# Delta-rule attention and a mixture of experts on one core: the expert stage in program order, with tokens fetched three tiles ahead and empty tiles behind branches

## The chip, the core and the metric

The kernel runs on one core of a Trainium2 chip. The core has five engines that run side by side: TensorE (PE, matrix products and transposes; its weight loads are shown apart as PEld), VectorE (DVE), ScalarE (ACT), GpSimd (POOL) and SyncE (SP), which here only issues transfers between the memory outside (DRAM) and the memory on the core. The metric is the device time of one execution in microseconds (us), as the median of several runs; lower is better.

## What is computed

There are two parts, one after the other. The first is attention by the delta rule, for 4 sequences of 768 tokens with 8 heads of width 48. The second sends each of the 4 x 768 = 3072 tokens (384 numbers each) to one of 8 experts and multiplies the result by a gate.

```python
# attention, for each sequence and head (state is 48 x 48)
k_n = k / (norm(k) + 1e-6)
for t in range(768):
    y[t] = q[t] @ state
    v_old = state.T @ k_n[t]
    state += beta[t] * outer(k_n[t], v[t] - v_old)
x = y with the heads side by side               # 3072 x 384

# experts: w1 is 8 x 384 x 1024, w2 is 8 x 1024 x 384, all float32
logits = (x / (norm(x) + 1e-6)) @ en.T / tau     # en: the expert vectors, normed
idx = argmax(logits);  gate = softmax(logits)[idx]
for e in range(8):
    m = idx == e
    out[m] = gate[m] * (maximum(x[m] @ w1[e], 0) @ w2[e])
```

With the reference's own inputs the experts get 385, 377, 351, 388, 365, 351, 421 and 434 tokens. In tiles of 128 tokens, each of one expert only, that makes 4 + 3 + 3 + 4 + 3 + 3 + 4 + 4 = 28 tiles.

## The kernel before

**Attention.** A sequence is cut into 12 chunks of 64 tokens; a unit is one chunk of two sequences (128 rows), so there are 24 units, number n = 2c + u. A unit's work is a list of steps, each with a place in a plan; a new unit starts every 20 places, so several are under way at once. PE, DVE, ACT and POOL run their instructions in the order of this plan.

**Routing.** The last steps of the plan find each token's expert, and write the token's number into that expert's list in DRAM (`idmap`). They are done for two chunks (G = 4 units, 512 tokens) at a time.

```python
    def route3(c, xc, ssx, lz):                     # place of each token in its expert's list
        oh = K["oh"]                                # oh: one-hot of the expert, 128 x G x E
        psR = K["psR"] = bank([128, G + 1, E])
        mm(psR, K["ones"][0:1, :], run.unsqueeze(1).broadcast_to([1, G + 1, E]))
        mm(psR[:, 0:G], K["mask_su"], oh, False)
        for g in range(G):
            mm(psR[:, g + 1:], K["ones"], oh[:, g:g + 1].broadcast_to([128, G - g, E]), False)
    # ... route4 makes slot_i and run (tokens so far of each expert) of psR;
    #     route5 and route6 make the gate and write x with it to x_dram

    def put_on_lists(g):                            # one such step for each of the G units
        def step(c, xc, ssx, lz):
            if g > 0:
                nc.gpsimd.memset(gap, 0.0)
            put = nc.gpsimd.indirect_dma_start(     # scatters 128 token numbers
                out=idmap[:, :], out_offset=bass.IndirectOffsetOnAxis(ap=K["slot_i"][:, g:g + 1], axis=0),
                in_=K["tokid"][:, c - 1 + g // NU, g % NU], in_offset=None)
            # ... the first of a group waits for those of the group before
```

**Experts.** The number of tiles of each expert is known only when the last tokens are routed, so `run` is turned into a table `info` of NT = 24 + 7 = 31 entries, the expert and the first list place of each tile, on one partition of DVE (some 20 small instructions). All 31 tiles are worked, those after the last used one with lists that hold only the number N, which names a row of zeros in x_dram and no row of the output.

```python
    def fetch(i):
        e = nc.values_load(info[0:1, 0, i:i + 1], engines=(SP,), min_val=0, max_val=E - 1)
        s = nc.values_load(info[0:1, 1, i:i + 1], engines=(SP,), min_val=0, max_val=NMAP - T)
        ids = mk.tile([128, ID], I32, name="ids", tag="ids", bufs=5)
        read = nc.sync.dma_start(ids, idmap[bass.ds(s, T), :])
        # ... after the last group's scatters into the lists
        w1 = wt.tile([128, KC, F], F32, name="w1", tag="w1")            # bufs=3
        nc.sync.dma_start(w1, moe_w1[bass.ds(e, 1)].rearrange("o (c p) f -> p (o c) f", p=128))
        w2 = wt.tile([128, NF, Dm], F32, name="w2", tag="w2")           # bufs=3
        nc.sync.dma_start(w2, moe_w2[bass.ds(e, 1)].rearrange("o (f p) m -> p (o f) m", p=128))
        x = mk.tile([128, ROW], F32, name="xg", tag="xg", bufs=5)
        nc.gpsimd.indirect_dma_start(out=x, ..., in_=x_dram[:, :], ...) # gathers 128 rows by ids
        return ids, w1, w2, x

    def transposed(x):                              # 3 transposes on PE, a copy on DVE
        ...
    def experts(xT, ids, w1, w2, x):
        hT = mk.tile([128, NF, T], F32, name="hT", tag="hT")
        for f in range(0, NF, 4):                   # NF = 8, KC = 3
            psH = acc([128, 4, T])
            for i in range(4):
                for j in range(KC):
                    nc.tensor.matmul(psH[:, i, :], lhsT=w1[...], rhs=xT[:, j, :], ...)
            nc.scalar.activation(hT[:, f:f + 4, :], psH, ACT.Relu)
        psO = acc([128, Dm])
        for f in range(NF):
            nc.tensor.matmul(psO, lhsT=hT[:, f, :], rhs=w2[:, f, :], ...)
        y = mk.tile([128, Dm], F32, name="y", tag="y", bufs=4)
        nc.vector.tensor_scalar_mul(y, psO, x[:, Dm:Dm + 1])
        nc.gpsimd.indirect_dma_start(out=out[:, :], ..., in_=y, ...)    # scatters 128 rows by ids

    ahead = [fetch(0), fetch(1)]
    xT = transposed(ahead[0][-1])
    for i in range(NT):
        now = ahead.pop(0)
        if i + 2 < NT:
            ahead.append(fetch(i + 2))
        nxT = transposed(ahead[0][-1]) if ahead else None
        experts(xT, *now)
        xT = nxT
```

In this text hidden(i) is the first product of tile i with its Relu, result(i) the second with its scaling and scatter, and w1(i), w2(i), ids(i), x(i) are what the tile reads.

Of the kernel before, what the change touches and what calls it, by code (L numbers as in the profile page):

```python
# [16 lines left out]
C = 64  # L17
# [5 lines left out]
def kernel(  # L23
# [53 lines left out]
    base_e = cpool.tile([1, E], F32, name="base_e")  # L77
    K = {}
# [181 lines left out]
    def late_constants3():  # L260
# [17 lines left out]
                          none.broadcast_to([128, NMAP * ID // 128 // NONE, NONE]))  # L278
        zrow = ac.tile([1, ROW], F32, name="zrow")
        nc.vector.memset(zrow, 0.0)  # L280
        nc.sync.dma_start(x_dram[N:N + 1, :], zrow)

# [22 lines left out]
    outs = {}  # L305
# [157 lines left out]
    def outputs(U):  # L463
        c, u = U["c"], U["u"]
        if u == 0 and c % 2 == 0:
            outs[c // 2] = (XC[c // 2 % 2],
                            wk.tile([128, 2, NU], F32, name="ssx", tag="ssx"),
                            wk.tile([128, 2, NU, E], F32, name="lz", tag="lz"))
        xc, ssx, _ = outs[c // 2]
        p = apply(U["M"], U["Z"])  # L470
        U["x"] = xc[:, c % 2, u, 0:Dm]
        xh = U["x"].rearrange("p (h d) -> p h d", h=H)
        if c > 0:
            nc.vector.tensor_tensor(xh, p, U["Yq"], op=ALU.add)
        else:
            nc.vector.tensor_copy(xh, p)
        ysq = wk.tile([128, Dm], F32, name="ysq", tag="ysq", bufs=1)
        nc.scalar.activation(ysq, U["x"], ACT.Square, accum_out=ssx[:, c % 2, u:u + 1])
# [8 lines left out]
    def logits(U):  # L487
        p = bank([128, E])
        for j in range(KC):
            for i in range(2):  # L490
                mm(p[HALF[i]], U["xT"][:, j, HALF[i]], enT[:, j, :], j == 0)
        nc.vector.tensor_copy(outs[U["c"] // 2][2][:, U["c"] % 2, U["u"]], p)

    G = 2 * NU
    ge = [128, G, E]

    def small(name, shape):
        return wk.tile(shape, F32, name=name, tag=name)

    def last_of_two_chunks(f):  # L500
        return lambda U: f(U["c"], *outs[U["c"] // 2]) if U["n"] % G == G - 1 else None

    def route1(c, xc, ssx, lz):

        ssx = ssx.rearrange("p o u -> p (o u)")
        nc.gpsimd.tensor_tensor(out=ssx, in0=ssx, in1=half.rearrange("p u h -> p (u h)")[:, 0:G], op=ALU.pow)
        lz = lz.rearrange("p o u e -> p (o u) e")
        m = small("m", [128, G])
        nc.vector.tensor_reduce(m, lz, axis=AX.X, op=ALU.max)
        K["el"] = small("el", ge)  # L510
        nc.vector.tensor_tensor(K["el"], lz, m.unsqueeze(2).broadcast_to(ge), op=ALU.subtract)

    def route2(c, xc, ssx, lz):

        pref = K["pref_e"].broadcast_to(ge)
        oh = K["oh"] = small("oh", ge)
        nc.vector.scalar_tensor_tensor(out=oh, in0=K["el"], scalar=0.0, in1=pref, op0=ALU.is_equal, op1=ALU.mult)
        best = small("best", [128, G])
# [3 lines left out]
    def route3(c, xc, ssx, lz):  # L522


        oh = K["oh"]
        psR = K["psR"] = bank([128, G + 1, E])
        mm(psR, K["ones"][0:1, :], run.unsqueeze(1).broadcast_to([1, G + 1, E]))
        mm(psR[:, 0:G], K["mask_su"], oh, False)
        for g in range(G):
            mm(psR[:, g + 1:], K["ones"], oh[:, g:g + 1].broadcast_to([128, G - g, E]), False)  # L530

    def route4(c, xc, ssx, lz):

        psR = K["psR"]
        rk = small("rk", ge)
        nc.vector.tensor_tensor(rk, psR[:, 0:G], K["oh"], op=ALU.mult)
        nc.vector.tensor_copy(run, psR[0:1, G])
        K["slot_i"] = wk.tile([128, G], I32, name="slot_i", tag="slot_i")
        slot = small("slot", [128, G])
        nc.vector.tensor_reduce(slot, rk, axis=AX.X, op=ALU.add)  # L540
        nc.vector.tensor_copy(K["slot_i"], slot)

    def route5(c, xc, ssx, lz):
        ssx = ssx.rearrange("p o u -> p (o u)")
        nc.vector.tensor_scalar_add(ssx, ssx, 1e-6)
        nc.vector.reciprocal(ssx, ssx)
        nc.vector.tensor_tensor(K["el"], K["el"], ssx.unsqueeze(2).broadcast_to(ge), op=ALU.mult)
        nc.scalar.activation(K["el"], K["el"], ACT.Exp)

    def route6(c, xc, ssx, lz):  # L550

        gate = xc.rearrange("p o u d -> p (o u) d")[:, :, Dm:Dm + 1]
        den = small("den", [128, G])
        nc.vector.tensor_reduce(den, K["el"], axis=AX.X, op=ALU.add)
# [3 lines left out]
        for o in range(2):  # L558
            t0 = (c - 1 + o) * C
            for i in range(2):  # L560
                nc.sync.dma_start(xd[i, t0:t0 + C], xc[HALF[i], o])
# [4 lines left out]
    def put_on_lists(g):  # L566
# [3 lines left out]
        def step(c, xc, ssx, lz):  # L570
            if g > 0:
                nc.gpsimd.memset(gap, 0.0)
            put = nc.gpsimd.indirect_dma_start(
                out=idmap[:, :], out_offset=bass.IndirectOffsetOnAxis(ap=K["slot_i"][:, g:g + 1], axis=0),
                in_=K["tokid"][:, c - 1 + g // NU, g % NU], in_offset=None)
            if g == 0:
                for other in lists[-G:]:
                    tc.add_manual_dep(put.ins, other.name, AFTER, reason="tokens' lists: two chunks after two others")
            else:
                tc.declare_no_dep(put.ins, group=f"lists{c}", reason="tokens' lists: distinct places")  # L580
            tc.add_to_no_dep_group(f"lists{c}", put.ins)
            lists.append(put.ins)
        return last_of_two_chunks(step)
# [14 lines left out]
        (79, x_transposes), (82, logits), (84, last_of_two_chunks(route1)), (87, last_of_two_chunks(route2)),  # L598
        (91, last_of_two_chunks(route3)), (94, last_of_two_chunks(route4)), (98, last_of_two_chunks(route5)),
        (103, last_of_two_chunks(route6)),  # L600
# [8 lines left out]
    ]  # L609
    steps = [(U["n"] * PERIOD + at, i, U["n"]) for U in UNITS for i, (at, _) in enumerate(PLAN) if i or U["n"]]  # L610
# [9 lines left out]
    wt = ctx.enter_context(tc.tile_pool(name="wt", bufs=3))  # L620
    mk = ctx.enter_context(tc.tile_pool(name="mk", bufs=2))
    pe = ctx.enter_context(tc.tile_pool(name="pe", bufs=1, space=bass.MemoryType.PSUM))

    def acc(shape):
        return pe.tile(shape, F32, name="acc", tag="acc", bufs=8)


    thr_i = cpool.tile([1, E, N // T], I32, name="thr_i")
    nc.gpsimd.iota(thr_i, pattern=[[0, E], [T, N // T]], base=0, channel_multiplier=0)
    thr = cpool.tile([1, E, N // T], F32, name="thr")  # L630
    nc.vector.tensor_copy(thr, thr_i)
    nth_i = cpool.tile([1, NT, 1], I32, name="nth_i")
    nc.gpsimd.iota(nth_i, pattern=[[1, NT], [0, 1]], base=0, channel_multiplier=0)
    nth = cpool.tile([1, NT, 1], F32, name="nth")
    nc.vector.tensor_copy(nth, nth_i)
# [4 lines left out]
    nc.vector.tensor_reduce(tiles[:, 0, :], thr, axis=AX.X, op=ALU.add)  # L640
    ends = cpool.tile([1, 1, E], F32, name="ends")
# [17 lines left out]
    nc.vector.tensor_copy(info[:, 1, :], begin)  # L659


    def fetch(i):
        e = nc.values_load(info[0:1, 0, i:i + 1], engines=(SP,), min_val=0, max_val=E - 1)
        s = nc.values_load(info[0:1, 1, i:i + 1], engines=(SP,), min_val=0, max_val=NMAP - T)
        ids = mk.tile([128, ID], I32, name="ids", tag="ids", bufs=5)
        read = nc.sync.dma_start(ids, idmap[bass.ds(s, T), :])
        for put in lists[-G:]:
            tc.add_manual_dep(read.ins, put.name, AFTER, reason="tokens' lists are complete")
        w1 = wt.tile([128, KC, F], F32, name="w1", tag="w1")
        nc.sync.dma_start(w1, moe_w1[bass.ds(e, 1)].rearrange("o (c p) f -> p (o c) f", p=128))  # L670
        w2 = wt.tile([128, NF, Dm], F32, name="w2", tag="w2")
        nc.sync.dma_start(w2, moe_w2[bass.ds(e, 1)].rearrange("o (f p) m -> p (o f) m", p=128))
        x = mk.tile([128, ROW], F32, name="xg", tag="xg", bufs=5)
        nc.gpsimd.indirect_dma_start(
            out=x, out_offset=None, in_=x_dram[:, :],
            in_offset=bass.IndirectOffsetOnAxis(ap=ids[:, 0:1], axis=0))
        return ids, w1, w2, x

    def transposed(x):
        xT = mk.tile([128, KC, T], F32, name="xTm", tag="xTm", bufs=3)  # L680
        psX = acc([128, KC, 128])
        for j in range(KC):
            nc.tensor.transpose(psX[:, j, :], x[:, j * 128:(j + 1) * 128], ident)  # L683
        nc.vector.tensor_copy(xT, psX)
        return xT

    def experts(xT, ids, w1, w2, x):
        hT = mk.tile([128, NF, T], F32, name="hT", tag="hT")
        for f in range(0, NF, 4):
            psH = acc([128, 4, T])  # L690
            for i in range(4):
                for j in range(KC):
                    nc.tensor.matmul(psH[:, i, :], lhsT=w1[:, j, (f + i) * 128:(f + i + 1) * 128], rhs=xT[:, j, :],  # L693
# [50 lines left out]
```

## Time and profile before

The time before is 832.64 us (median of 3 runs, 830.83 to 836.68). The profiled execution spans 831.9 us from the first to the last instruction, with a mean granted TensorE clock of 0.970 of full speed.

| engine | busy us | share of the span | instructions |
|---|---|---|---|
| PE | 731.6 | 88% | 15196 |
| PEld | 622.3 | 75% | 15196 |
| DVE | 280.3 | 34% | 632 |
| ACT | 243.8 | 29% | 468 |
| POOL | 226.7 | 27% | 260 |

A row of a group in the profile reads: line, engine, operation, what it writes <- what it reads, size, count; then busy time in all, mean ns of one, idle time of the engine just before these instructions and what ended it. The rows of 40 digits cut the span into 40 slices of 20.8 us; a digit is the busy share in tenths. In the timeline a row is: start in us, duration in us, engine, line, operation, what it writes <- what it reads, count, and in brackets the idle time before and what ended it. "DMA" rows count the 16 transfer engines of the core; "landing" is when a transfer is complete. A float32 matrix product shows as two records in PE's rows.

### The profile page before, as it was taken

The numbers are of one execution on the slowest core, as the hardware profiler recorded it, in microseconds if no ns is written. First come the engines' busy times: TensorE is split into PE (matmuls) and PEld (weight loads), VectorE is DVE, ScalarE is ACT, GpSimd is POOL, SyncE is SP. The second block draws the span as 40 slices with busy tenths as digits, with TensorE's granted clock in tenths as the row PEclk, the third lists the DMA queues.
The fourth block names the chain that finished last, engine by engine and source line by source line (L and its number), as shares of the span: only waits on it lengthen the run. The fifth ranks groups of instructions, "written<-read, shape, count | busy, mean of one in ns | idle before, by whom it ended". The sixth has DMA issues, their size and how long they took to land. (4 is left out here: it accounts for less than half of the span.)

```text
span 831.9 us, 33270 instructions
## 1 busy us (share of the span) xinstructions
PE 731.6 (88%) x15196; PEld 622.3 (75%) x15196; DVE 280.3 (34%) x632; ACT 243.8 (29%) x468; POOL 226.7 (27%) x260
## 2 busy tenths in 40 slices
PE   3589989999999989999886079999999999999995
PEld 2478878888888888888775067778888887777784
DVE  5565555555555655555432201100111111111000
ACT  3445444454445444454332001111111101101110
POOL 5543224433433433441200211111111111111110
PEclk9999999999999999999988579999999999999998
DMA  6344211321312321110010799999999999999920
GB/s 114 58 120 76 42 32 33 84 51 33 74 34 45 70 52 24 22 46 5 5 44 2 258 360 329 330 329 321 329 329 324 322 312 337 330 316 331 336 98 0
DMA packets 134957, 132.19 MB, mean 159 GB/s; under 512 B 84154, under 2 KB 119393, under 8 KB 134818
## 3 DMA queue, kind: packets, MB, share of 16 engines
q1 hardware_dynamic: 129874, 118.76, 46.9%
q0 software_dynamic: 4736, 11.27, 3.6%
q8 instruction: 119, 1.95, 1.0%
q14 instruction: 20, 0.16, 0.1%
q10 hardware_dynamic: 208, 0.05, 0.0%
HBM read 118.39 MB, written 13.04 MB: 158 GB/s over the span
## 5 line engine op out<-in xcount | busy, mean ns | idle before, releaser
L693 PE MATMUL acc<-xTm,w 128*128 128x128 f32 x1488 | 173.5, 277 | 0.0
L693 PEld LDWEIGHTS acc<-xTm,w 128*128 128x128 f32 x1488 | 171.0, 194 | 0.3
L698 PE MATMUL acc<-w,hT 128*128 128x384 f32 x496 | 165.1, 486 | 0.0
L698 PEld LDWEIGHTS acc<-w,hT 128*128 128x128 f32 x496 | 91.9, 190 | 57.5
L695 ACT ACTIVATE hT<-acc 128x512 f32<-128x512 f32 x62 | 37.0, 597 | 323.1 <-PE acc L693 291.9
L700 DVE TENSOR_SCALAR y<-acc,xg 128x384 f32<-128x384 f32 x31 | 19.1, 618 | 305.6 <-PE acc L698 305.6
L701 POOL DMA_INDIRECT out_dram<-y,ids x31 | 31.6, 1018 | 270.4 <-DVE y L700 270.4
L398 DVE COPY_PREDICATED P<-below,pair 128x512 f32<-128x512 int32 x96 | 70.0, 731 | 49.4 <-PE pair L308 42.2
L308 PE MATMUL pair<-W,P 64*64 64x64 f32 x3072 | 75.5, 224 | 12.5 <-issue 8.0
L384 ACT ACTIVATE W<-pair 128x512 f32<-128x512 f32 x96 | 57.5, 599 | 91.9 <-PE pair L308 86.5
L308 PEld LDWEIGHTS pair<-W,P 64*64 64x64 f32 x3072 | 64.3, 136 | 17.5 <-issue 11.4
L323 POOL TENSOR_TENSOR rn<-rn,half 128x8 f32<-128x8 f32 x24 | 39.5, 1644 | 137.1 <-DVE rn L322 103.9
L308 PE MATMUL bank<-Z,G 64*64 64x48 f32 x1536 | 57.9, 220 | 7.3 <-issue 5.9
L308 PE MATMUL bank<-R,W 64*64 64x48 f32 x1536 | 56.2, 218 | 6.6 <-issue 4.5
L308 PEld LDWEIGHTS bank<-Z,G 64*64 64x64 f32 x1536 | 51.8, 136 | 8.3 <-issue 5.9
L308 PEld LDWEIGHTS bank<-R,W 64*64 64x64 f32 x1536 | 51.2, 135 | 8.8 <-issue 8.2
L368 PE MATMUL bank<-ident,W 128*128 128x128 f32 x288 | 47.9, 289 | 1.3 <-ACT W L384 1.2
L308 PE MATMUL pair<-T,AJ 64*64 64x64 f32 x1536 | 39.0, 226 | 9.9 <-DVE T L376 7.0
L362 POOL TENSOR_TENSOR G<-G,upper 128x512 f32<-128x512 f32 x24 | 30.9, 1287 | 37.2 <-ACT G L356 36.2
L308 PEld LDWEIGHTS pair<-T,AJ 64*64 64x64 f32 x1536 | 31.7, 135 | 12.2 <-DVE T L376 7.8
L683 PEld LDWEIGHTS acc<-ident,xg 128*128 128x128 f32 x93 | 12.3, 145 | 36.4 <-issue 23.5
L683 PE MATMUL acc<-ident,xg 128*128 128x128 f32 x93 | 16.0, 283 | 26.5 <-DMA xg<-x_dram,ids 26.5
(161 smaller groups left out, 879.4 us busy)
## 6 DMA issues: line engine op xcount, KB each, us to landing
w<-in_moe_w_dram SPq DMA_DIRECT2D x62, 1536.0 KB
x_dram<-XC SPq DMA_DIRECT2D x24, 200.0 KB
k_in<-in_k_dram SPq DMA_DIRECT2D x48, 96.0 KB
QQ<-in_q_dram SPq DMA_DIRECT2D x48, 96.0 KB
v_in<-in_v_dram SPq DMA_DIRECT2D x48, 96.0 KB
idmap<-none SPq DMA_DIRECT2D x1, 1792.0 KB
ids<-idmap SPq DMA_DIRECT2D x31, 8.0 KB
xg<-x_dram,ids POOLq DMA_INDIRECT x31
```

What stands on the lines that cost most here:

```text
L308: nc.tensor.matmul(out_, lhsT=lhsT, rhs=rhs, start=start, stop=True, skip_group_check=True)
L323: nc.gpsimd.tensor_tensor(out=U["rn"], in0=U["rn"], in1=half[:, 0], op=ALU.pow)
L362: nc.gpsimd.tensor_tensor(M, M, upper.broadcast_to(hc), op=ALU.mult)
L368: nc.tensor.transpose(p[:, j].rearrange("p r c -> p (r c)"), src[:, j].rearrange("p r c -> p (r c)"), ident)
L384: nc.scalar.activation(out_, in_, ACT.Copy)
L398: nc.vector.copy_predicated(U["P"], below[s].broadcast_to(jc), p)
L683: nc.tensor.transpose(psX[:, j, :], x[:, j * 128:(j + 1) * 128], ident)
L693: nc.tensor.matmul(psH[:, i, :], lhsT=w1[:, j, (f + i) * 128:(f + i + 1) * 128], rhs=xT[:, j, :], start=(j == 0), stop=(j == KC - 1))
L695: nc.scalar.activation(hT[:, f:f + 4, :], psH, ACT.Relu)
L698: nc.tensor.matmul(psO, lhsT=hT[:, f, :], rhs=w2[:, f, :], start=(f == 0), stop=(f == NF - 1))
L700: nc.vector.tensor_scalar_mul(y, psO, x[:, Dm:Dm + 1])
L701: nc.gpsimd.indirect_dma_start(out=out[:, :], out_offset=bass.IndirectOffsetOnAxis(ap=ids[:, 0:1], axis=0), in_=y, in_offset=None, bounds_ ...
```

## The change

The change is in the order and the timing of the work between the last routing steps and the end. Each expert tile that is worked does the same arithmetic as before.

1. **The last two chunks are routed one by one** (groups of 2, 2, 2, 2, 2, 1, 1 chunks). The last group has then two units, and two scatters into the lists, where it had four.
2. **Weights of expert 0 are loaded during attention**, into buffers that are never shared with attention's, by 14 transfers of 192 or 256 KB, one for each unit's 20 places of the plan from place 100 on. Tile 0 is taken to be expert 0's first tile (the number of tiles of expert 0 is at least 1 now), so its list place needs no table.
3. **Two constant tables** of the count (`thr`, `nth`) are made during attention.
4. **The whole expert stage is in program order** on every engine, SP's transfers too, with buffers taken in turn from rings. ids are read five tiles ahead, x three tiles ahead, w1(i + 3) is asked for after hidden(i) and w2(i + 3) after result(i). PE's order is hidden(i), transposes of tile i + 1, result(i).
5. **The first weights from DRAM**, w1(1), are asked for only once x(0) has landed.
6. **Empty tiles behind branches**: tiles 0 to 23 are always worked, 24 to 27 only if more than 24 tiles are used, 28 to 30 only if more than 28 are. Every engine loads the number of used tiles into a register.

```diff
+    w1_first = cpool.tile([128, KC, F], F32, name="w1_first")
+    w2_first = cpool.tile([128, NF, Dm], F32, name="w2_first")
...
+    def first_weights(i):
+        if i < NF:
+            nc.sync.dma_start(w2_first[:, i], moe_w2[0, i * 128:(i + 1) * 128])
+        else:
+            c, f = (i - NF) // 2, (i - NF) % 2 * (F // 2)
+            nc.sync.dma_start(w1_first[:, c, f:f + F // 2], moe_w1[0, c * 128:(c + 1) * 128, f:f + F // 2])
...
+    groups, group_of = [], []
+    while len(group_of) < NC:
+        chunks = 1 if len(group_of) >= NC - 2 else 2
+        groups.append(dict(n=len(groups), first=len(group_of), chunks=chunks))
+        group_of += chunks * groups[-1:]
...      (route1 to route6 and put_on_lists work on a group g of G = 2 * chunks units)
+    events += [(PERIOD * (5 + i), lambda i=i: first_weights(i)) for i in range(NF + 2 * KC)]
...
+    ctx.enter_context(tc.manual_schedule())
...
+    w1_ring = ring("w1_", 3, [128, KC, F], first=[w1_first])
+    w2_ring = ring("w2_", 3, [128, NF, Dm], first=[w2_first])
+    ids_ring, x_ring = ring("ids", 7, [128, ID], I32), ring("xg", 6, [128, ROW])
...      (where, read_ids, read_x, read_w1, read_w2, transposed, hidden, result: fetch and experts in pieces)
+    where(work[0], 0)                    # no table: e = 0, s = 0
+    work[0].w1, work[0].w2 = w1_ring(), w2_ring()
+    read_ids(work[0])
+    read_x(work[0])
...      (the table info is made of run, as before)
+    nc.vector.tensor_scalar_max(tiles[:, :, 0], tiles[:, :, 0], 1.0)
...
+    for i in range(1, 5):
+        where(work[i], i)
+        read_ids(work[i])
+        if i == 1:
+            tc.add_manual_dep(read_w1(work[i]).ins, work[0].read.ins.name, AFTER, reason="first tokens, then weights")
+            read_w2(work[i])
+        if i < 3:
+            read_x(work[i])
+    read_w1(work[2])
+    read_w2(work[2])
+    transposed(work[0])
+    count = nc.values_load(used[0:1, 0:1], min_val=0, max_val=NT)
+
+    def work_through(first, last):
+        for i in range(first, last):
+            if i + 3 < NT:
+                read_x(work[i + 3])
+            hidden(work[i])
+            if i + 3 < NT:
+                read_w1(work[i + 3])
+            if i + 1 < NT:
+                transposed(work[i + 1])
+            result(work[i])
+            if i + 3 < NT:
+                read_w2(work[i + 3])
+            if i + 5 < NT:
+                where(work[i + 5], i + 5)
+                read_ids(work[i + 5])
+
+    parts = [N // T, N // T + E // 2, NT]
+    work_through(0, parts[0])
+    with tc.If(count > parts[0]):
+        work_through(parts[0], parts[1])
+        with tc.If(count > parts[1]):
+            work_through(parts[1], parts[2])
...
-    ahead = [fetch(0), fetch(1)]
-    xT = transposed(ahead[0][-1])
-    for i in range(NT):
-        ...
```

## Prediction

> **What bounds the kernel now.** I read the page's rows of 40 slices first, for the stages:
>
> ```profile
> PE   3589989999999989999886079999999999999995
> PEclk9999999999999999999988579999999999999998
> DMA  6344211321312321110010799999999999999920
> ```
>
> There are two stages with a hole between them. In slices 0 to 21 (attention, to about 455 us) PE is busy and the transfer engines have much room; slice 22 (458 to 478 us) has no matrix product at all; from there to the end PE is at 9 and the transfers are at 9 too. The change touches the hole and the second stage, so I cut these into windows (window in us, its length, then busy us and count for each engine, PE clock, DMA share, GB/s):
>
> ```profile
> 464.00:468.00 4.00, 0.00 (x0) 0.00 (x0) 0.00 (x0) 0.00 (x0) 0.36 (x1) 0.50 0.41 99
> 468.00:474.00 6.00, 0.00 (x0) 0.00 (x0) 0.00 (x0) 0.00 (x0) 0.63 (x1) 0.50 1.04 401
> 483.00:496.35 13.35, 13.35 (x70) 11.18 (x69) 0.58 (x2) 1.19 (x2) 0.94 (x1) 0.81 1.05 387
> 496.35:821.90 325.55, 325.12 (x2007) 259.72 (x2005) 32.05 (x59) 35.83 (x60) 1.00 0.89 300
> ```
>
> From 496.35 us on PE has 325.12 us of work in 325.55: it is the bound there, with 30 tiles, 10.85 us each. The transfers run at 300 GB/s against 387 to 401 when they are behind, so they are near the bound but not on it. The timeline gives the hole's steps and one steady tile:
>
> ```profile
> 456.68 1.04 POOL L573 DMA_INDIRECT idmap<-tokid,slot_i  x1 [4.84 <-DVE ssx L545]
> 458.02 0.95 POOL L573 DMA_INDIRECT idmap<-tokid,slot_i  x1 [0.21 <-issue]
> 459.28 0.96 POOL L573 DMA_INDIRECT idmap<-tokid,slot_i  x1 [0.22 <-issue]
> 460.55 0.96 POOL L573 DMA_INDIRECT idmap<-tokid,slot_i  x1 [0.22 <-issue]
> 464.55 0.38 SPq L666 DMA_DIRECT2D ids<-idmap  x1
> 467.64 0.98 POOL L674 DMA_INDIRECT xg<-x_dram,ids  x1 [6.14 <-issue]
> 474.04 0.88 PE L683 MATMUL acc<-ident,xg 128*128 128x128 f32 x3 [18.35 <-DMA xg<-x_dram,ids]
> 482.64 0.90 PE L683 MATMUL acc<-ident,xg 128*128 128x128 f32 x3 [7.72 <-DMA xg<-x_dram,ids]
> 483.33 7.80 PE L693 MATMUL acc<-xTm,w 128*128 128x128 f32 x48
> ...
> 507.31 5.52 PE L693 MATMUL acc<-xTm,w 128*128 128x128 f32 x48
> 512.66 5.33 PE L698 MATMUL acc<-w,hT 128*128 128x384 f32 x16
> ...
> 816.76 5.33 PE L698 MATMUL acc<-w,hT 128*128 128x384 f32 x16
> ...
> 823.02 0.98 POOL L701 DMA_INDIRECT out_dram<-y,ids  x1 [9.51 <-DVE y L700]
> ```
>
> The hole is a chain: four scatters into the lists, 1.27 us apart; the last ends at 461.5 and lands about 3 us later, which releases ids(0) at 464.55; x(0) is gathered from 467.64 and reaches PE at 474.04, 6.4 us, while four weight transfers fill the DMA (share 1.04). Then PE has x(0) but stands in program order before the transposes of x(1), which come at 482.64. So hidden(0) begins at 483.33, 31.3 us after the last logits are copied (452.05). At the other end the last product is done at 822.1, and SP's waits show what follows (engine, line, what it waited for: us in total, times, longest):
>
> ```profile
> SPq L739 <- DMA out_dram<-y,ids: 34.7, 1, 34.7
> SPq L739 <- PEq L739: 6.1, 2, 5.6
> ```
>
> SP issued its last transfer at about 790.3, so the last scatter lands near 825.0, 3 us after PE; the remaining 6.9 us to 831.9 are the common end.
>
> [...] clock 0.50 in the hole, hidden(0) takes 7.80 us where a steady one takes 5.52. The new kernel will pay this once too. [...] Here the list scatters land in 3.1 us (median); the shorter last group thus saves the issue of two scatters and no landing. [...]
>
> **The change part by part.**
>
> *Empty tiles.* 28 tiles are used. No expert's count lies just under a multiple of 128 (377 is nearest to 384 from below), so rounding cannot make a 29th; 385 and 388 could at most drop one. "More than 24" is true, "more than 28" is false: tiles 28 to 30 fall away, 3 x 10.85 = **-32.6 us** of PE time in the stage where PE is the bound.
>
> *Routing.* Two scatters fewer: -2 x 1.27 = -2.5. Of route3's twelve records for four units (0.65 + 0.64 + 1.85 us) half of the eight of 1.85 go: -0.9. Against it, chunk 10's own routing falls into the draining attention: some 14 DVE instructions of about 0.2 us and 8 PE records. DVE is a fifth busy there (2.13 of the 10 us from 440), so I charge 1 us, not their sum of 3. Net -2.4: ids(0) at about 462.1.
>
> *ids(0) needs no table.* The table was ready at about 461.7, before the scatters had landed, so this alone is worth nothing; in program order the table's instructions now come after the gate's, end near 463, and delay only ids(1), which is not urgent.
>
> *x(0) alone on the DMA.* ids(0) to gather 3.1 as before: 465.2. The gather without weights beside it: 205 KB, a link like the scatters, so I estimate 3.5 instead of 6.4: x(0) at 468.7. Transposes 0.9 and copy 0.6 as at 474.04 to 475.56: hidden(0) can begin at **470.2**, since its weights are there and no x(1) stands before it: 13.1 earlier than 483.33. The register load of the count lies in PE's order between the transposes and hidden(0), beside the copy.
>
> *Tile 0* takes 13.1 us as before (483.33 to 496.45), as the clock is low again: hidden(1) at 483.3. w1(1) and w2(1), 3.1 MB from 468.7 at 387 GB/s, take 8.1 us: there at 477 to 478, in time. w1(2) and w2(2) follow by 487, needed from 494. In the steady state a weight buffer is asked for again at the same point as before (w1 after hidden of the tile that used it) and needed 27 us later, as before. So no gain and no loss from the ring; x is one tile earlier.
>
> *Steady tiles.* Same products, another order; PE was never waiting, so 10.85 stays. Tiles 1 to 27 end at 483.3 + 325.6 - 32.6 = 776.3.
>
> *Branches.* Two compares, the second behind PE's last work: +1.
>
> *End.* w1(30) and w2(30) are asked for although tile 30 is not worked; w2(30) only after result(27), just when y goes out. 1.5 MB at 387 GB/s are 4.1 us beside the last scatter. Contended scatters land in 7.2 us (median of all 31; lowest 3.0): **+4.2**.
>
> *Loads during attention.* 3.1 MB more, over some 250 us in which the DMA is about 20% busy: 0.
>
> Sum: 831.9 - 13.1 - 32.6 + 1 + 4.2 = 791.4 for the profiled span. The timed runs lie 0.7 above it (832.64 against 831.9): **792**.
>
> **Rivals.**
> 1. *The branches hold all engines together.* If each block begins only when earlier work is done, PE would lose its lead at tile 24[...]. For it: nothing inside a branch can be moved ahead of it[...]. Against: each engine has the number in its own register, and needs no other engine to decide.
> 2. *The transfers become the bound.* With PE 13 us earlier and the first weights asked for later (468.7 instead of 465.2), tiles 1 to 3 could wait. For it: the DMA share is 0.89 even in the steady part, and small gathers then land late. Against: 3.1 MB per 10.85 us is 290 GB/s, and 387 was reached. Two or three waits of 2 us: 796 to 798.
> 3. *The chain is longer than I think at its start.* If chunk 10's routing holds up unit 23 by its full 3 us, or its scatters hold the first of the last group: 794 to 796.
> 4. *The end is free.* If the unused weights don't slow the scatter, and x(0) lands in 2.5 us: 787.
>
> **Range and chances.** The sure part is the skipped tiles; the start has four estimates of 1 to 2 us each, the end one of 4, the branches one of 0 to 10. That is why the range reaches farther up: 784 to 803. The -32.6 alone is 3.9%; to lose the 2%, stalls of 29 us would be needed, which only a slower steady tile (+1 us each) could make. Faster 0.95, same 0.03, slower 0.02.
>
> **What would show it.** Right: L573's last scatter near 458; x(0) at PE near 469; the first product of the experts near 470 with the clock at 0.5; 28 pairs of products, 10.85 us apart, without idle PE at tile 24; the last near 776; the last scatter landing some 7 us after it. Wrong: an idle PE ahead of the first product of tile 24 (rival 1); PE waiting for w in tiles 1 to 3 (rival 2); the last logits later than 453 (rival 3); 31 tiles worked.

## The result, and the profile after

| | before | after |
|---|---|---|
| device time, median of 4 runs each, us | 832.43 | 799.98 |
| ratio, with its 95% interval | 1 | 0.9606 (0.9555 to 0.9657) |
| span of the profiled run, us | 831.9 | 798.6 |

The change makes the kernel 3.9% faster: 32.5 us, where 40 were predicted. The rows of 40 slices of the changed kernel (20 us each):

```profile
PE   2578899998999998999988729999999999999993
PEclk9699999999999999999999658999999999999997
DMA  6336422321142131111001029999999999999996
```

The hole has not gone. It is at slice 23 and ends at 480 us, only 3.6 us earlier than before, and PE's clock is already down in slice 22, while attention still works. The copy of the last logits, before and after:

```profile
452.05 0.17 DVE L492 COPY lz<-bank 128x8 f32<-128x8 f32 x1 [2.04 <-PE bank L308]
```

```profile
463.25 0.17 DVE L511 COPY lz<-bank 128x8 f32<-128x8 f32 x1 [2.40 <-PE bank L325]
```

From there on the timeline of the changed kernel has the same steps as the one shown of before:

```profile
468.26 0.96 POOL L605 DMA_INDIRECT idmap<-tokid,slot_i  x1 [0.21 <-issue]
...
472.21 2.41 SPq L692 DMA_DIRECT2D ids<-idmap  x2
474.72 0.99 POOL L698 DMA_INDIRECT xg<-x_dram,ids  x1 [5.49 <-DMA ids<-idmap]
...
478.12 0.87 PE L714 MATMUL acc<-ident,xg 128*128 128x128 f32 x3 [12.16 <-DMA xg<-x_dram,ids]
...
479.70 7.71 PE L723 MATMUL acc<-xTm,w_first 128*128 128x128 f32 x48 [0.70 <-DVE xTm L715]
...
492.73 5.52 PE L723 MATMUL acc<-xTm,w 128*128 128x128 f32 x48
...
780.45 5.33 PE L730 MATMUL acc<-w_first,hT 128*128 128x384 f32 x16
...
786.71 1.02 POOL L733 DMA_INDIRECT out_dram<-y,ids  x1 [8.56 <-DVEq L806]
```

From these rows and the same ones of before, each link, in us:

| link | before | after | difference | predicted |
|---|---|---|---|---|
| start to last logits copied | 452.05 | 463.25 | **+11.2** | +1.0 |
| last logits to ids(0) asked for | 12.5 | 9.0 | -3.5 | -3.4 |
| ids(0) to the gather of x(0) | 3.1 | 2.5 | -0.6 | 0 |
| gather to the transposes of tile 0 | 6.4 | 3.4 | -3.0 | -2.9 |
| transposes to hidden(0) | 9.3 | 1.6 | -7.7 | -7.8 |
| hidden(0) to hidden(1) | 13.1 | 13.0 | -0.1 | 0 |
| hidden(1) to the last product | 325.6 | 293.05 | -32.6 | -32.6, and +1 for branches |
| last product to the end | 9.8 | 12.8 | +3.0 | +4.2 |
| sum | 831.9 | 798.6 | -33.3 | -40.5 |

All links of the hole and of the expert stage came out within 0.6 us of what was worked out (the one us for branches aside, which is not there), the end at 3.0 us instead of 4.2. One link did not: attention's last logits are 11.2 us late, ten more than was charged. The experiments are about that, and about the 3 us of the end.

### The profile page after: what moved, and what is told of

The parts are those of the page before. It is cut to its first block, busy times and chain, and to the rows that moved or that the text cites. A ratio compares the mean times of both kernels' runs of the same rounds, so it can differ in the third digit from the quotient of the medians.

```text
span 798.6 us, 32885 instructions
## 1 busy us (share of the span) xinstructions
PE 705.7 (88%) x15002; PEld 603.9 (76%) x15002; DVE 281.7 (35%) x644; ACT 240.6 (30%) x463; POOL 223.9 (28%) x257
## 3 DMA queue, kind: packets, MB, share of 16 engines
q8 instruction: 119, 1.95, 1.0%
## 4 chain that ended last, share of the span: by engine, by line
PE 58%; DMA 17%; issue 12%; DVE 6%; ACT 5%; SPq 0%; POOL 0%; POOLq 0%; ACTq 0%; DVEq 0%
PE pair L325 19%; DMA out_dram<-y,ids 16%; PE bank L325 15%; PE acc L723 8%; PE acc L730 7%; PE bank L385 6%; ACT G L373 2%; PE bank L360 1%; PE bank L501 1%; ACT W L401 1%; DVE P L415 1%; DVE W L376 1%; ACT KT L401 1%; DVE XC L492 1%; PE acc L714 1%
## 5 line engine op out<-in xcount | busy, mean ns | idle before, releaser
L725 ACT ACTIVATE hT<-acc 128x512 f32<-128x512 f32 x56 | 33.5, 598 | 279.9 <-PE acc L723 264.7
L723 PEld LDWEIGHTS acc<-xTm,w 128*128 128x128 f32 x864 | 99.3, 192 | 4.8
L723 PE MATMUL acc<-xTm,w 128*128 128x128 f32 x864 | 99.4, 275 | 0.0
L730 PE MATMUL acc<-w,hT 128*128 128x384 f32 x288 | 95.9, 486 | 0.0
L733 POOL DMA_INDIRECT out_dram<-y,ids x28 | 28.5, 1017 | 228.6 <-DVE y L732 211.5
L325 PE MATMUL pair<-W,P 64*64 64x64 f32 x3072 | 75.6, 224 | 13.3 <-issue 8.3
L730 PEld LDWEIGHTS acc<-w,hT 128*128 128x128 f32 x288 | 53.3, 190 | 33.4
L715 DVE COPY xTm<-acc 128x384 f32<-128x384 f32 x29 | 16.2, 558 | 151.9 <-PE acc L714 151.9
L723 PEld LDWEIGHTS acc<-xTm,w_first 128*128 128x128 f32 x480 | 57.2, 198 | 3.5 <-DVE xTm L715 1.1
L723 PE MATMUL acc<-xTm,w_first 128*128 128x128 f32 x480 | 57.4, 281 | 0.7 <-DVE xTm L715 0.7
L730 PE MATMUL acc<-w_first,hT 128*128 128x384 f32 x160 | 53.3, 486 | 0.0
L325 PE MATMUL pair<-T,AJ 64*64 64x64 f32 x1536 | 40.5, 228 | 11.1 <-DVE T L393 7.0
```

Of the source, the lines that this page charges most:

```text
L325: nc.tensor.matmul(out_, lhsT=lhsT, rhs=rhs, start=start, stop=True, skip_group_check=True)
L715: nc.vector.tensor_copy(t.xT, psX)
L723: nc.tensor.matmul(psH[:, i, :], lhsT=t.w1[:, j, (f + i) * 128:(f + i + 1) * 128], rhs=t.xT[:, j, :], start=(j == 0), stop=(j == KC - 1))
L725: nc.scalar.activation(t.hT[:, f:f + 4, :], psH, ACT.Relu)
L730: nc.tensor.matmul(psO, lhsT=t.hT[:, f, :], rhs=t.w2[:, f, :], start=(f == 0), stop=(f == NF - 1))
L733: nc.gpsimd.indirect_dma_start(out=out[:, :], out_offset=bass.IndirectOffsetOnAxis(ap=t.ids[:, 0:1], axis=0), in_=y, in_offset=None, bound ...
```

## Experiments

All runs of one group were on one chip; the groups are e1 to e4, the changed kernel again to e7, and e8 to e11. The kernel before took 821.0, 818.9 and 835.2 us on their chips, so ratios to it are compared, not times. Attention also differs from trace to trace of one program: the logits of unit 19 came at 405.2 us in one trace of the changed kernel and at 388.6 in another, on another chip. Therefore the traces are compared over short stretches. The stretches of all traces, in us ("clock falls": how long before the last logits the last halving of PE's clock ahead of them begins). In the traces of the kernel before and of the changed one every stretch at one clock, apart from the last, is a whole multiple of 3.41 us long (before: 6.83 us from 416.41 at 0.50, then 27.31 at 1.00, then 37.55 at 0.50, so 2, 8 and 11 of them); two traces whose clock falls 3 us apart can differ by one such step.

| kernel | logits of unit 1 | unit 21 to 23 | clock falls | last logits to ids(0) | hidden(0) to (1) | end | ratio |
|---|---|---|---|---|---|---|---|
| before | 93.6 | 14.4 | 1.5 | 12.5 | 13.1 | 9.8 | 1 |
| after | 96.4 | 21.9 | 16.7 | 9.0 | 13.0 | 12.8 | 0.9606 |
| e1 pairs | 99.3 | 15.1 | 3.9 | 12.0 | 12.8 | 11.8 | 0.9544 |
| e2 weights in the hole | 93.4 | 21.0 | 15.4 | 8.9 | 13.6 | 12.3 | 0.9563 |
| e3 no unused weights | 98.9 | 21.6 | 16.8 | 9.0 | 12.9 | 11.0 | 0.9569 |
| e4 all tiles | 99.0 | 21.0 | 15.4 | 9.0 | 13.7 | 9.8 | 0.9900 |
| after again | 96.1 | 21.3 | 16.3 | 9.0 | 13.2 | 12.9 | 0.9603 |
| e5 pairs, spread | 92.7 | 15.6 | 5.0 | 12.0 | 13.9 | 11.9 | 0.9506 |
| e6 filled drain | 96.1 | 19.5 | 13.1 | 8.4 | 13.3 | 12.5 | 0.9548 |
| e7 all of it | 94.1 | 17.9 | 9.7 | 12.7 | 11.0 | 11.0 | 0.9481 |
| e8 moved routing | 99.0 | 18.1 | 8.5 | 9.0 | 13.7 | 12.2 | 0.9550 |
| e9 pairs, best | 92.9 | 16.7 | 8.5 | 12.0 | 12.5 | 11.0 | 0.9497 |
| e10 moved, best | 93.5 | 18.1 | 8.3 | 9.0 | 11.0 | 11.0 | **0.9447** |
| e11 no branch | 97.6 | 21.7 | 16.4 | 9.0 | 13.2 | 9.6 | (one run) |

### e1: the last two chunks routed together again

```diff
-        chunks = 1 if len(group_of) >= NC - 2 else 2
+        chunks = 2
```

> The changed kernel with its last two chunks routed together again (last group 4 units, 4 scatters). Theory R (chunk 10's own routing, put into PE's and DVE's order of the draining attention, costs more than the two scatters save): the last logits are copied near 456 to 458 instead of 463.25, because the 8 route records and the PSUM bank they hold no longer stand ahead of units 22 and 23; from there to ids(0) 12.5 us as in the kernel before instead of 9.0; sum about 796 to 798. Theory C (the clock fell by chance of its window, routing or not): last logits near 463 still, and 3.5 us later ids(0): 803 to 804. Either way the halving of the clock relative to the last logits shows in the trace: C says some 16 us before them again, R says at most 5 us before.

Measured: ratio 0.9544 (0.9504 to 0.9584). Units 21 to 23 take 15.1 us instead of 21.9, and the clock falls 3.9 us before the last logits instead of 16.7. The way from there to ids(0) is 3.0 us longer. So routing the last chunks one by one costs 6.8 us and brings 3.0: this part of the change loses some 4 us by the traces. (Against e2 to e4, on e1's own chip, it costs 5.9 to 6.5 us.) The ratio points the same way, by 5 us, but its interval and the changed kernel's overlap. The two traces show how. First the timeline of the kernel before, PE alone:

```profile
440.81 1.10 PE L308 MATMUL bank<-Z,G 64*64 64x48 f32 x32
441.77 1.14 PE L308 MATMUL bank<-R,W 64*64 64x48 f32 x32
```

and the same two groups (the output of unit 22, the first solve of unit 23) in the changed kernel, with the route products of chunk 10 ahead of them:

```profile
444.67 0.40 PE L325 MATMUL bank<-run,ones 1*128 1x24 f32 x2
...
445.76 1.32 PE L325 MATMUL bank<-Z,G 64*64 64x48 f32 x32
...
447.74 0.14 DVE L567 COPY run<-bank 1x8 f32<-1x8 f32 x1
...
447.88 1.95 PE L325 MATMUL bank<-R,W 64*64 64x48 f32 x32 [0.80 <-DVE run L567]
```

The first group waits for the route products in PE's order. The second needs a PSUM bank; there are two, and the route's result holds one until DVE has read it, which in DVE's order comes after unit 22's output. The solve starts 2.1 us after the output's products instead of 1.0. From the logits of unit 21 to this solve it is 6.5 us instead of 4.2: +2.3. Then the same 32 records take 1.95 us instead of 1.14: at 446.55 the clock was halved, and the remaining 15.4 us to the last logits had taken 10.3 before: +5.1. Sum 7.4, the whole difference between 14.4 and 21.9. Of the 5.1 us, 4.3 are PE's own records, busy for 11.12 us instead of 6.87; the other 0.8 are longer waits.

### e2: tile 0's weights loaded in the hole

```diff
-    events += [(PERIOD * (5 + i), lambda i=i: first_weights(i)) for i in range(NF + 2 * KC)]
...
-    work[0].w1, work[0].w2 = w1_ring(), w2_ring()
     read_ids(work[0])
+    read_w1(work[0])
+    read_w2(work[0])
```

> The changed kernel with tile 0's weights not loaded during attention, but asked for right after ids(0), as in the kernel before. Theory D (those 14 transfers, which all ran between 63 and 89 us, are what makes attention 3.8 us later at unit 20): logits of unit 20 near 401.5 instead of 405.2, and the lost head start costs 3 to 6 us in the hole: 799 to 802. Rival (attention is late by its clock and by chance, the transfers are free): unit 20 near 404 to 406 still, hidden(0) begins 3 to 6 us later than in the changed kernel: 803 to 806.

(The figures 401.5 and 405.2 of this text belong to unit 19.) Measured: ratio 0.9563 (0.9529 to 0.9597), not told apart from the changed kernel's; it makes 796 of 832.4 us, below both forecasts. Unit 1's logits come at 93.4 us instead of 99, unit 19's at 390.5, against 396.4 to 402.6 in e1, e3 and e4 on the same chip. From ids(0) to hidden(0) it is 11.0 us instead of 7.5: the gather of x(0), which now has weights beside it, takes 6.7 us of it instead of 3.4. So the early weights bring 3.5 us in the hole, and unit 1 is 5.5 us later with them (3.0 in the changed kernel's own trace): as done here, that part of the change shows no gain. Theory D holds at unit 1. That its delay lasts to the end of attention is not shown, as the second group has unit 19 both early and late with the same loads (see e5).

### e3, e4, e11: the end and the branches

e3 asks for the weights of tiles 28 to 30 only inside the last branch; e4 works all 31 tiles without branches; e11 is e3 with 28 tiles in line, and leaves tiles 28 to 30 out altogether.

```diff
     # e3
-            if i + 3 < NT:
+            if i + 3 < last or last < parts[1]:
                 read_w1(work[i + 3])       # and read_w2 in the same way
...
         with tc.If(count > parts[1]):
+            for t in work[parts[1]:]:
+                read_w1(t)
+                read_w2(t)
     # e4
-    work_through(0, parts[0])
-    with tc.If(count > parts[0]):
-    ...
+    work_through(0, NT)
```

> The changed kernel, but the weights of tiles 28 to 30 are asked for inside the last branch, so that no unused ones are read. Theory (w2(30) beside the last scatter makes the end 12.8 us instead of 9.8): the end from the last product to the last instruction falls to about 10, total 797 to 798. Rival (the end is longer for the branch or because this scatter really writes 50 rows): the end stays at 12 to 13 us, 800.

> The changed kernel without branches: all 31 tiles are worked, in line. Theory (the skipped tiles give their full 3 x 10.85 us and the branches cost nothing): 800 + 32.6 - about 2 to 3 (no unused weights at the end) = 829 to 831. If the branches cost something, the difference to the changed kernel is smaller by it: each us of branch cost lowers this figure by one. It is also a second sample of the same attention: last logits near 463 if the routing does it, 455 to 460 if the clock fell by chance.

> e3 (no unused weights) without branches, working 28 tiles in line; it leaves out tiles 28 to 30 altogether, so it is right for these inputs only. It parts the 11.0 us of e3's end: if they hold 1.2 us for the branches, the end is 9.8 as in the kernel of 31 tiles in line; if that is the last scatter, which here writes 50 rows and there none, it stays at 11.0. From hidden(1) to the last product 293.0 us in both cases, if the branch on the way costs PE nothing.

Measured: the end is 12.8 us in the changed kernel, 11.0 in e3, 9.6 in e11, and 9.8 in e4 and before, whose last scatter writes no row. So the unused weights cost 1.8 us, the branches 1.4, both at the end, and writing 50 rows costs nothing that shows. (Over all traces with branches the end is 11.8 to 12.9 us with the unused weights and 11.0 without, so that their cost is 0.8 to 1.9.) e3's ratio of 0.9569 (0.9538 to 0.9599) is not told apart from the changed kernel's; the 1.8 us are read from the traces. On PE the branches cost nothing: hidden(1) to the last product takes 293.05 us with them (the changed kernel) and without (e11). e4's ratio is 0.9900 (0.9846 to 0.9954): without the skipped tiles the rest of the change is worth 1%. From hidden(1) on its 30 tiles take 325.3 us, 32.2 more than the 27 of the others. (That 0.9900 lies a little below the 0.996 to 0.998 which the expected 829 to 831 us make of 832.4. Against e3, on the same chip, e4's median is 30.2 us higher, where the traces make 31.0: 32.2 for the tiles less 1.2 at the end.)

The unused weights hold up the last transfers by more than they lengthen the end. SP's last waits (engine, line, what it waited for: us in total, times, longest), in the changed kernel and in e3:

```profile
SPq L833 <- DMA out_dram<-y,ids: 7.5, 2, 5.4
SPq L833 <- PEq L833: 3.3, 2, 2.8
```

```profile
SPq L836 <- PEq L836: 6.8, 2, 6.2
```

SP has seen its last transfers land 9.3 us after the last product in the changed kernel and 4.1 in e3, so 5.2 us later. But behind that it waits 2.8 us for the other engines, and in e3 6.2. GpSimd's closing instruction, a drain, runs beside the transfers, from 3.0 us after the last product to 11.7 in the changed kernel and to 9.9 in e3. In e11 it runs from 0.7 to 8.8: with the branches GpSimd first has an instruction of theirs that takes 1.85 us. So the 6.9 us which the prediction took for a common end do not all stand behind the last landing.

### after again, e5 and e6: where the loads stand, and how busy PE is

The changed kernel was run once more as the measure of its group. e5 is e1 with the 14 loads issued by ACT, which works in plan order; SP, on which they stood, does not during attention. e6 is the changed kernel with idle products (of the identity with itself, their result unused) between the last steps of attention.

```diff
     # e5, in first_weights (and chunks = 2)
-            nc.sync.dma_start(w2_first[:, i], ...
+            nc.scalar.dma_start(w2_first[:, i], ...
     # e6
+    def filler(n):
+        t = pair([1, 128])
+        for _ in range(n):
+            mm(t[:, 0, 0], ident, ident)
+    events += [(at, lambda: filler(3)) for at in (510, 516, 520, 526, 534, 540, 546)]
```

> The changed kernel itself once more, on the same chip as the three others, as their measure. If routing and loads act as the first four runs suggest, its trace shows again a clock halved some 15 to 17 us before the last logits, and 21 to 22 us from the logits of unit 21 to those of unit 23. Ratio to the kernel before 0.957 to 0.961.

> Routing in pairs as in e1, and the 14 loads of tile 0's weights issued by ACT, at their places in ACT's plan order, so that they are spread over attention and don't stand before the q, k and v loads in SP's queue. Theory D (bunched at 63 to 89 us, they hold up q, k, v, and PE's clock falls for it): the logits of unit 1 come at about 93.5 as in e2 and not at 99, those of unit 19 some 5 to 8 us earlier than in e1, and the hole is as short as in e1: 5 to 8 us below e1, so 8 to 13 us below the changed kernel on the same chip. Rival (it is the 3.1 MB, not the place, that costs): the delay is only moved to later units, unit 19 as late as in e1, within 2 us of e1.

> The changed kernel with seven pieces of three idle 128 x 128 products (of the identity, their result unused) put into PE's order between the steps of units 22 and 23. Theory C2 (single routing is dear because PE's thin work lets the clock be halved early): the clock stays up longer, unit 21 to unit 23 takes 16 to 18 us instead of 21 to 22, in spite of 21 products of 0.22 us more; total 3 to 6 us below the changed kernel. Rival (the steps of routing themselves and the PSUM bank they hold are what costs, the clock only follows): 21 to 22 us or more still, total equal or up to 4 us above.

Measured: the changed kernel 0.9603 (0.9574 to 0.9633), with its clock and its units 21 to 23 as expected; e5 0.9506 (0.9473 to 0.9539), e6 0.9548 (0.9519 to 0.9576). SP's timeline in the changed kernel shows what e5 mends: of the 14 loads, meant for one in every 20 places of the plan, 11 went out in two bunches, and all between 63 and 89 us.

```profile
71.15 4.35 SPq L296 DMA_DIRECT2D w_first<-in_moe_w_dram  x6
...
83.56 1.28 SPq L122 DMA_DIRECT2D QQ<-in_q_dram  x2
84.89 3.54 SPq L299 DMA_DIRECT2D w_first<-in_moe_w_dram  x5
```

After the second bunch PE stops in the middle of a group of products. The same 23 records in PE's timeline of e1, where the stop is longest, and of e5:

```profile
94.20 0.57 PE L325 MATMUL pair<-W,P 64*64 64x64 f32 x23 [3.30 <-issue]
```

```profile
89.05 0.57 PE L325 MATMUL pair<-W,P 64*64 64x64 f32 x23 [0.83 <-issue]
```

In the eight traces with bunches this stop takes 1.4 to 3.3 us (1.9 in the changed kernel's first trace), in the six without 0.6 to 1.1. "issue" means that PE waits for nothing the profile knows of: no data, no other engine. In the changed kernel's trace one packet of 16384 bytes in the instruction queue runs from 90.37 to 91.32 us, and PE goes on at 92.73; whether PE waited for it, and whether the weights held it up, is not shown. PE also has such stops without loads of weights: seven of 0.25 to 0.48 us between 414 and 419 us in the kernel before, with the transfers at a share of 0.06. In e1, e3, e4, e8 and e11 the clock is then halved for 6.8 to 10.2 us from 92 to 96 us on, and unit 1's logits come at 97.6 to 99.3. With the same bunches but no halving there (both traces of the changed kernel, and e6) they come at 96.1 to 96.4; with spread loads or none (before, e2, e5, e7, e9, e10) at 92.7 to 94.1. So the bunches cost 2 to 4 us at unit 1, and a fall of the clock that can follow another 1 to 3. Whether that delay lasts isn't shown: on the chip of this group unit 19's logits come at 388.6 and 398.3 us with the bunches (the changed kernel again, e6) and at 393.6 and 394.8 with spread loads (e5, e7). In time e5 is 3 us below e1 in ratio (0.0038 of 821), in the direction of theory D and short of its 5 to 8, with intervals that overlap; it isn't settled. Below the changed kernel of its own chip e5 is by 8 us (0.0097 of 819), the low end of the 8 to 13 expected, with intervals apart; but it differs from that in its routing too.

e6 holds the clock longer, as hoped, but not throughout: it is halved for 6.8 us from 437.2 and comes back, and units 21 to 23 take 19.5 us instead of 21.3. Less than predicted there, but in time 3.2 us below the changed kernel of its group (783.26 against 786.45), the low end of what was expected, with intervals that just overlap. Neither theory's figure for units 21 to 23 was met.

### e8: single routing that keeps out of the way

```diff
+        if g["chunks"] == 1:
+            psR = g["psR"] = pair([2 * NU + 1, E])[:, 0, 0:G + 1]      # route3; else a bank, as before
...
-        (91, last_of_group(route3)), (94, last_of_group(route4)), ...
+        (91, last_of_group(route3, (2,))), (94, last_of_group(route4, (2,))),
+        (94.6, last_of_group(route3, (1,))), (97.6, last_of_group(route4, (1,))), ...
     # the second argument: for groups of how many chunks the step is done
```

> The changed kernel, single routing kept, but chunk 10's place products moved behind the first solve of unit 23 (plan 514.6 instead of 511), their reading on DVE behind the second solve (517.6 instead of 514), and their PSUM taken from the three pair buffers, which are idle by then, instead of one of the two banks that the solves need. Theory R2 (PE's order and the held bank cost the first 2.3 us, and the thin work they cause makes the clock fall early, which costs the other 5): unit 21 to 23 takes 15 to 17 us instead of 21 to 22, the last logits to ids(0) 9.0 us still, total 4 to 7 us below the changed kernel (ratio 0.952 to 0.956). Rival (any PE route work in the drain brings the clock down): 20 to 22 us still, ratio 0.958 to 0.961.

Measured: ratio 0.9550 (0.9495 to 0.9605), not told apart from the changed kernel's by itself. PE's timeline of e8:

```profile
444.53 1.10 PE L325 MATMUL bank<-Z,G 64*64 64x48 f32 x32
445.49 1.14 PE L325 MATMUL bank<-R,W 64*64 64x48 f32 x32
446.55 0.40 PE L325 MATMUL pair<-run,ones 1*128 1x24 f32 x2
```

Output and solve stand 1.0 us apart again. Units 21 to 23 take 18.1 us against 21.7 in e11 on the same chip, and the clock falls 8.5 us before the last logits instead of 16.4. e9 (below), which routes in pairs on the same chip, takes 16.7 us, with the clock falling 8.5 us before them too. So the order and the bank, which were changed together, make 3.7 of the 5.0 us between e11 and e9, and the early fall of the clock came with them. The other 1.3 lie between the solve of unit 23 and the logits of unit 22, where chunk 10's products now stand: 6.5 us instead of 5.1. That these products also bring the clock down earlier than pairs do is not shown: it falls 3.9 and 5.0 us before the last logits in e1 and e5, but 8.5 in e9. The 15 to 17 us expected were not reached; the ratio lies in the range expected.

### e7, e9, e10: the pieces put together

All three have spread loads and no unused weights, and idle products before the transposes of tile 0 (44 in e7 and e9, 36 in e10). e7 routes in pairs and has three fillers of e6, e9 is e7 without these, e10 routes as e8.

```diff
+    warm = acc([128, 128])
+    for _ in range(36):
+        nc.tensor.matmul(warm, lhsT=ident, rhs=ident, start=True, stop=True)
     transposed(work[0])
```

> Meant as the best: e5, no unused weights as in e3, three pieces of idle products at the end of attention, and 44 idle products between the last routing and the transposes of tile 0, so that PE's clock is up when hidden(0) begins. If the clock holds, hidden(0) takes 5.5 to 6 us instead of 7.7 and the routing's products 1 us less: 3 to 5 us below e5, of which 1 is from the end. If the idle products don't raise the clock in time or stand before the transposes too long, equal to e5 or 1 to 4 us above.

> e7 without its three pieces of idle products in attention's end (they seem to have lengthened it: 17.9 us from unit 21 to 23 where pairs otherwise take 14.4 to 15.6): pairs, spread loads, no unused weights, 44 idle products before the transposes of tile 0. Unit 21 to 23 in 14.5 to 16 us, hidden(0) to hidden(1) in 11 us instead of 13: 1 to 3 us below e7, ratio 0.945 to 0.948. If the pieces did no harm, the ratio stays at 0.948 or above.

> e9 with single routing as moved in e8 (and 36 idle products, the hole being shorter). If e8's move works: 2 to 3 us below e9, as the last logits to ids(0) take 9.0 instead of 12.2; ratio 0.942 to 0.946. If it does not, 2 to 4 us above e9.

Measured: e7 0.9481 (0.9454 to 0.9508), e9 0.9497 (0.9445 to 0.9549), e10 0.9447 (0.9392 to 0.9502). e7 is 2.4 us below e5 in its median (777.27 against 779.68), where 3 to 5 were expected, and their intervals overlap. e7 and e9 are not told apart, so whether the three pieces did harm stays open. Nor are e9 and e10, so whether moved single routing beats pairs stays open too. e10 took 791.28 us where the kernel before took 835.24: by its ratio it beats both kernels. Its PE timeline in the hole:

```profile
460.69 10.95 PE L788 MATMUL acc<-ident 128*128 128x128 f32 x72 [0.42 <-DVE slot L572]
...
473.63 5.62 PE L727 MATMUL acc<-xTm,w_first 128*128 128x128 f32 x48 [0.70 <-DVE xTm L719]
```

The idle products fill 10.95 us in which PE had nothing to do, and hidden(0) takes 5.62 us instead of 7.71. In e7, e9 and e10 PE's clock is back at full 4.5 to 6.0 us after the first idle product. In e10 they end 0.8 us before the transposes, in e9 1.4 us before; there the clock fell for 3.4 us at 481.7, just when hidden(0) began, and hidden(0) to hidden(1) took 12.5 us instead of 11.0.

## Why the prediction was right, and where it was wrong

It said 792, range 784 to 803; the time is 800.0. The time lies in the range and the mechanism of the gain was right; it is 8 us above the middle, by one term of the sum. That it lies in the range is partly luck: the range reached up to 803 for the branches (put at 0 to 10 us as an estimate, from no trace), which cost 1.4 us, while the ten us came from steps that were charged 1 and 0. The prediction's own sign for this, last logits later than 453, was there: 463.25. By its steps:

- *Empty tiles, -32.6*: right. 28 tiles were worked, and 27 of them take 293.05 us. PE has 264.00 us of work in the 264 from 496 to 760 us, so nothing of it was lost.
- *ids(0), gather, transposes* (-14.1 for these links): right, measured -14.8; the estimate of 3.5 us for the gather alone was 3.4.
- *"Routing ... I charge 1 us, not their sum of 3"*: this is the step that failed. Together with "Loads during attention: 0" it predicted +1.0 where +11.2 was measured. The runs put in its place: 7.4 us between units 21 and 23 from single routing, of which 2.3 are waiting (PE's order and a held PSUM bank) and 5.1 come behind it, where the clock was halved 15 us too early. The other 3.8 are there by unit 21. At unit 1 the kernel is 2.8 us late (96.4 against 93.6), which the bunched loads do; that these 2.8 us lasted to unit 21 is not shown, and the cause of the rest stays open. I had counted busy time on engines that had room, but a chain in which each link waits for the one before pays for what stands in its order, not for the room.
- *Tile 0, steady tiles*: right, 13.0 and 10.85 us.
- *Branches, +1* (an estimate of mine, from no trace): right, though 1.4: none on PE in front of tile 24, and all of it at the end.
- *End, +4.2*: right for the transfers, which landed 5.2 us later for the unused weights, and wrong for the end, of which these weights are only 1.8: the 6.9 us behind the landing were not a fixed sum. With 1.4 for the branches that makes the 3.0 measured, to within 0.2.
- *The clock*: that it would be low again held, with 0.50 in the hole and hidden(0) at 7.71 us, and mattered more than I used it. I charged the low clock to hidden(0) alone, not to attention's end, where it was 0.50 from 446.55 us on.

Of the rivals, the first and the second are out: PE keeps its pace at tile 24 (293.05 us from hidden(1) to the last product, with the branch and without), and with the transfers at a share of 0.96 it still never waits. The third named the right place, the routing of chunk 10, and made 794 to 796 of it, where it alone took 7.4 us. The fourth is out too: the end is 3.0 us longer, and the gather took 3.4 us, not 2.5.

## What to carry to other kernels

Work that is moved off the last step into a stage that is draining isn't free because the engines there have room: look at what stands ahead of it in each engine's order, at the buffers that it holds, and at whether PE keeps its clock. A transfer placed in a plan goes out where its own queue puts it (here 11 of 14 in two bunches, at 71 and 85 us); if that queue isn't held to the plan, look in the trace where it went. Skipping work in the stage that one engine bounds gave its full time here (32.6 us for three tiles of 10.85), and the branch for it cost that engine nothing (293.05 us with it and without).

## What the runs showed of the hardware that I had not expected

- Of two stretches, PE's clock was halved behind the busier one. In the kernel before, PE was busy 4.90 of the 6.83 us from 436.88 on and kept its full clock until 450.54; in the changed one it was busy 5.70 of the 6.83 us up to 446.55, and there the clock was halved. Most records in both are small (64 x 48 and 64 x 64, in the changed one also 16 to 24 columns for routing); what the clock follows is not shown. All six traces with unmoved single routing and no fillers have the clock falling 15.4 to 16.8 us before the last logits, the four with pairs and no fillers in attention 1.5 to 8.5, the two with moved single routing 8.3 and 8.5.
- With idle products of 128 x 128 the clock was back at full 4.5 to 6.0 us after the first of them (e7, e9, e10). In e10 that was within the hole: its mean from 457.6 to 473.6 us is 0.73, where the changed kernel has 0.50 from 463.4 to 479.7. From hidden(0) to hidden(1) it is 11.0 us where they end 0.7 or 0.8 us before the transposes (e7, e10), 12.5 where they end 1.4 us before (e9) and 12.8 to 13.9 without them. No run changed them alone, so what they are worth in the whole time is not shown.
- PE can stop without any wait on data that the profile shows: 3.3 us behind bunched loads (e1), against 0.8 at the same records with the loads spread (e5). What it waits for is not shown.
